# The 32-row tail matmuls of split products on 128 rows, 32 of them with zero weights, in place of 96 rows

## The chip, the cores and the metric

The kernel runs on one core of one Trainium2 chip. The metric is the device time of one execution in microseconds. Before the change it is 1619.23 us, the median of three runs (1618.24 to 1619.66).

## The reference

`x` is 2048 x 576. A layer norm gives `xn`; two branches work on it, and the result is `x + s * silu(b)`.

```python
xn = _layernorm(x, axis=-1)
s = _A_ref(xn, A_wqkv, A_w_phi, A_wo)
g = _silu(_B_ref(xn, B_w_gate, B_w_up, B_w_down))
return x + s * g
```

`_A_ref` is linear attention with 32 heads of 18 columns: `q`, `k` and `v` by one product with `wqkv` (576 x 1728); a feature map for `q` and `k`, which is a small product per head and two softmaxes of it, of both signs; then `phi_q (phi_k^T v)` over a denominator, and a product with `wo` (576 x 576). `_B_ref` is a gated feed-forward part: `(silu(xn @ w_gate) * (xn @ w_up)) @ w_down`, with 4608 hidden columns.

## The kernel before

**Split products.** Each float32 operand is held as a high part, rounded to the type float32r in which TensorE multiplies, and a low part, the rest. A product is then three matmuls: high by high, high by low, low by high. The contraction runs over 576 = 4 x 128 + 64 rows. The kernel cuts it into two blocks `k`, each with two chunks of 128 rows and a tail of 32. A chunk takes three matmuls. A tail takes one: its 32 rows are laid out three times, one copy under the other, with the parts so arranged (the high part in two groups of 32 rows and the low part in the third, on either side in a different group) that one matmul on 96 rows sums the three products. The layout in memory has a fourth copy, in rows 96 to 127, which no matmul reads. So a product of one block is 7 matmuls: six on 128 rows and, as the last, the tail on 96.

**Where tails stand.** Three helpers issue them:
- `xw` (L84 to L95) for the projections to `q`, `k` and part of `v`, and for the early tiles of the feed-forward part (`early_tile`, L121). It goes through both blocks `k`, so one tail is in the middle of an accumulation and one at its end: for each block L87 to L90 list six pairs, L91 the tail, and L94 issues all.
- `v_product` (L412 to L418) for the rest of `v`.
- `product` (L749 to L753) for the gate and up products. `b` is a part of `x` as the moving operand, 512 columns; the weights are the stationary one.

**The feed-forward part** takes most of the time. A unit is one tile of 128 hidden columns for one half of the rows of `x`. Its gate and up products on two blocks of rows are done by a scheme of seven products in place of eight (`gate_up`, L774), each with `product`: `px`, `py` and `pw` (at the start also `pd`) are the PSUM banks they accumulate in. Between products `fill()` (L1087) issues pieces of the down projection, 6 or 12 matmuls of 288 columns each (`three`, L866 to L871), which write `pd`. `gate_up_weights` (L712) brings the weights of a unit: SP loads `ld` (L720), ScalarE and VectorE split it (`split`, L59 to L61), GpSimd forms sums; in the second half of the rows the split weights come back from memory (`w_dram`). The tails of a unit's seven products, already split, come from `t_dram` into the tile `wt`, 96 rows by 7 x 128 (L736). `wt` is taken from the pool `fw` at each unit, from two buffers in turn (L714).

**Order of the work.** The program is written as a whole, and a scheduler places each instruction on its engine's list by its own estimates; `high_priority` and `issue_after` steer it. In the last stretch of the attention part, the projection by `wo` (`project`, L634, matmuls of L650) and the last early tile (L94) share TensorE, and VectorE forms the low parts `ol` that L650 reads (L61). The pool `fw` is opened after this part in the code, and its tiles lie where tiles of the attention part were, so their first writers wait for the last readers of those.

Of the kernel before, what the change touches and what calls it, by code (L numbers as in the profile page):

```python
# [9 lines left out]
F32 = mybir.dt.float32  # L10
F32R = mybir.dt.float32r
# [7 lines left out]
P = 128  # L19
# [29 lines left out]
def gated_hedgehog_kernel(ctx: ExitStack, tc, x, w_qk, w_v, w_phi, wo, w_gu, w_tail, w_down, ident_in, mask_in, out):  # L49
# [5 lines left out]
    nc = tc.nc  # L55
# [3 lines left out]
    def split(hi, lo, src):  # L59
        nc.scalar.copy(hi, src)  # L60
        nc.vector.tensor_sub(lo, src, hi)  # L61
# [15 lines left out]
    t_dram = dram.tile([TAILS, 4, 3, 32, 7, P], F32, name="t_dram")  # L77
# [6 lines left out]
    def xw(ps, i, j, cols, wh, wl, stationary_x):  # L84
        pairs = []
        for k in range(2):
            b = XB[i][2 * j + k]  # L87
            for c in range(2):
                pairs += [(b[:, c, cols], w[:, k, c]) for w in (wh, wl)]
                pairs += [(b[:, 3 + c, cols], wh[:, k, c])]  # L90
            pairs += [(b[0:96, 2, cols], wh[0:96, k, 2])]  # L91
        for n, (a, b) in enumerate(pairs):
            l, r = (a, b) if stationary_x else (b, a)
            last = nc.tensor.matmul(ps, l, r, start=n == 0, stop=n == len(pairs) - 1)  # L94
        return last  # L95
# [8 lines left out]
    def early_weights(f, *behind):  # L104
        parts = []
        for m in (0, 2):
            raw = epool.tile([P, 2, 3, P], F32, name="raw", bufs=2)
            hi = epool.tile([P, 2, 3, P], F32R, name="wh", bufs=3)
            lo = epool.tile([P, 2, 2, P], F32R, name="wl", bufs=3)
            nc.sync.dma_start(raw, w_gu[f, :, m:m + 2])  # L110
            with ExitStack() as order:
                for b in behind:
                    order.enter_context(tc.issue_after(b.ins))
                with tc.high_priority():
                    rests.append(split_rows(hi, lo, raw))
            parts.append((hi, lo))
        return parts
# [19 lines left out]
    with ExitStack() as att:  # L137
# [17 lines left out]
        with ExitStack() as wst:  # L155
# [245 lines left out]
            def xs(k, n):  # L401
                if n < 4:
                    b, cs = XB[k // 4][n], slice(k % 4 * P, (k % 4 + 1) * P)
                    return [b[:, c, cs] for c in range(5)]
                j = n - 4
                h = his[k, j // 2 * 2]
                return [h[:, j % 2, c] for c in range(3)] + [los[k][:, j, c] for c in range(2)]
# [4 lines left out]
            def v_product(ps, x, w, first, last):  # L412
                wh, wl = vws[w]
                mm = [m for c in range(2) for m in ((x[c], wh[:, c]), (x[c], wl[:, c]), (x[3 + c], wh[:, c]))]
                mm += [(x[2][0:96], wh[0:96, 2])]
                for n, (l, r) in enumerate(mm):
                    nc.tensor.matmul(ps[:, 0:HALF], l, r, start=first and n == 0, stop=last and n == len(mm) - 1,
                                     skip_group_check=True)  # L418
# [44 lines left out]
            for p in range(8):  # L463
                k = (p + 4) % 8
# [26 lines left out]
                x = [xs(k, n) for n in range(8)]  # L491
# [186 lines left out]
        for f, halves in [(1, (0,)), (0, (0,))] + [(f, (1, 0)) for f in range(2, EARLY)]:  # L678
            parts = first_weights.pop() if f == 1 else early_weights(
                f, *{0: read[2 * NT + 1:2 * NT + 2], 2: (read[2 * NT + 3], exps[NT + 1])}.get(f, ()))  # L680
# [3 lines left out]
    fw = ctx.enter_context(tc.tile_pool(name="fw", bufs=1))  # L684
    fp = ctx.enter_context(tc.tile_pool(name="fp", bufs=1, reuse_waits="tile"))
    acc = fp.tile([P, 4, HT // 2, HALF], F32, name="acc")

    def operands(i):

        xo = [None] * 7  # L690
        for n in (0, 6, 3, 1, 5, 4, 2):
            if n < 3:
                j = (0, 1, 3)[n]
                if i:
                    t = xpool.tile([P, 5, BT], F32R, name=f"X0{j}")
                    nc.sync.dma_start(t.bitcast(F32), a_dram[n])
                else:
                    t = XB[0][j]
                xo[n] = [t[:, c] for c in range(5)]
                continue  # L700
            j = n - 3
            t = xpool.tile([P, 5, BT], F32R, name=f"X1{j}")
            parts = 1 if i else 4
            rows = t.bitcast(F32).rearrange("p c n -> p (c n)").rearrange("p (a m) -> p a m", a=parts)
            src = sum_dram[i, :, j].rearrange("p s c n -> p (s c n)").rearrange("p (a m) -> p a m", a=parts)
            for a in range(parts):
                nc.sync.dma_start(rows[:, a], src[:, a])
            v = t.rearrange("p c n -> p (c n)").rearrange("p (s c n) -> p s c n", s=4, c=5)
            xo[n] = [v[:, :, c] for c in range(5)]
        return xo  # L710

    def gate_up_weights(i, f):  # L712

        parts, wt = {}, fw.tile([96, 7, P], F32R, name="wt", bufs=2)  # L714
        n, q = divmod(f - EARLY, 4)
        raw = i == 0 or f < FIRST[0]
        if raw:
            ld = fw.tile([P, 2, D], F32, name="ld", bufs=2).rearrange("p a b -> p (a b)")
            ld = ld[:, 0:8 * P].rearrange("p (m c n) -> p m c n", m=4, c=2)
            nc.sync.dma_start(ld, w_gu[f, :, :, 0:2])  # L720
            ts = fw.tile([P, D], F32, name="ts")[:, 0:4 * P].rearrange("p (m c n) -> p m c n", m=2, c=2)

        def ready(m, src):
            k = 1 if m == 6 else 2
            w = fw.tile([P, k, 4, P], F32R, name=f"w{k}", bufs=2 if k == 1 else 4)
            if not raw:
                nc.sync.dma_start(w.bitcast(F32), w_dram[f - EARLY, :, m:m + k])
            else:
                split(w[:, :, 0:2], w[:, :, 2:4], src)
                if i == 0 and f < NF - 1:  # L730
                    nc.sync.dma_start(w_dram[f - EARLY, :, m:m + k], w.bitcast(F32))
            for c in range(k):
                parts[m + c] = w[:, c]

        ready(0, ld[:, 0:2] if raw else None)
        nc.sync.dma_start(wt.bitcast(F32), t_dram[n, q].rearrange("b r m n -> (b r) m n"))  # L736
        if raw:
            nc.gpsimd.tensor_sub(ts[:, 0], ld[:, 2], ld[:, 0])  # L738
            nc.gpsimd.tensor_sub(ts[:, 1], ld[:, 3], ts[:, 0])
            nc.gpsimd.tensor_sub(ld[:, 2], ld[:, 3], ld[:, 2])  # L740
            nc.gpsimd.tensor_sub(ld[:, 1], ld[:, 1], ts[:, 1])  # L741
        ready(4, ts if raw else None)
        ready(2, ld[:, 2:4] if raw else None)
        held = {0: silus[-2:-1], 2: tops[0:1], 3: tops[1:2]}.get(f - FIRST[0]) if i == 0 else None
        with tc.issue_after(held[0].ins) if held else ExitStack():
            ready(6, ld[:, 1:2] if raw else None)
        return parts, wt

    def product(ps, w, m, b, first, last):  # L749
        mm = [(w[0][m][:, i], b[j]) for c in range(2) for i, j in ((c, c), (2 + c, c), (c, 3 + c))]  # L750
        mm += [(w[1][:, m], b[2][0:96])]
        for n, (l, r) in enumerate(mm):
            nc.tensor.matmul(ps, l, r, start=first and n == 0, stop=last and n == len(mm) - 1, skip_group_check=True)  # L753

# [19 lines left out]
    def gate_up(w, xo, fill, opening):  # L774
# [26 lines left out]
        def top(s2):  # L801
            with tc.high_priority():
                anchor.append(nc.vector.tensor_mul(h[0], yp, s2))  # L803

        product(xp, w, 0, A11, True, False)
        with tc.high_priority():
            copies.append(nc.scalar.copy(yp, xp))  # L807
        product(wp, w, 4, S1, True, False)
        if opening < 2:
            product(xp, w, 5, S2, False, False)  # L810
            s2 = snap(xp)
            product(yp, w, 1, A12, False, True)
            silu_y()
            product(xp, w, 2, S3, False, False)
            s3 = snap(xp)
            add(wp, s3)
            add(wp, s2)
            zp = fps.tile([P, 2, 512], F32, name="pd", bufs=2)[:, 0]
            product(zp, w, 3, S4, True, True)
            add(zp, s2)  # L820
            top(s2)
            product(xp, w, 6, A22, False, True)
            silu_x(s3)
            return h
# [274 lines left out]
    parts = early_weights(EARLY)  # L1099
# [11 lines left out]
    for i, n, f in units:  # L1111
# [3 lines left out]
        if f >= FIRST[i]:  # L1115
            w = kept.pop() if i and kept else ready.pop(0)
# [33 lines left out]


def chunks(w):
    tails = [np.broadcast_to(w[512 + 32 * k:544 + 32 * k], (4, 32, w.shape[1])).reshape(P, -1) for k in range(2)]
    return np.stack([np.stack([w[256 * k:256 * k + P], w[256 * k + P:256 * k + 2 * P], tails[k]], 1)
                     for k in range(2)], 1)

# [25 lines left out]
```

## Time and profile before

| what | before |
|---|---|
| median of three runs | 1619.23 us |
| span of the profiled execution, first to last instruction | 1616.8 us |
| time of that execution beside the span | not given by the profile; the median is 2.4 us above the span |
| busy: PE, weight loads, VectorE, ScalarE, GpSimd | 99%, 88%, 72%, 45%, 41% |
| granted TensorE clock, mean | 0.999 |
| DMA, mean | 166 GB/s |

PE stands for matmuls and PEld for the weight loads that overlap them. Records of matmuls overlap each other as well: a matmul's record lasts longer than the time until the next one starts. The span divides roughly into preparation and attention up to 485 us, the first half of the feed-forward part up to some 1040 us, and the second half.

### The profile page before, as it was taken

What the parts mean: (1) busy time and instruction counts of PE and PEld (TensorE: products, weight loads), DVE (VectorE), ACT (ScalarE), POOL (GpSimd) and SP (SyncE); (2) the same over time, 40 slices, a digit from 0 to 9 for tenths busy, and PEclk for the clock granted to TensorE, in tenths of its full rate; (3) what the DMA queues carried; (4) which work ended last, traced back from release to release, by engine and by line L of the source; (5) the groups of instructions that cost most, each with busy time, mean ns of one, the idle gap of its engine ahead of it and who ended that gap; (6) DMA issues with size and microseconds to landing.
All of it is one profiled execution on the core that took longest, in us unless ns stands there. A gap on an engine that the chain in (4) does not pass through costs nothing.

```text
span 1616.8 us, 25312 instructions
## 1 busy us (share of the span) xinstructions
PE 1606.6 (99%) x9415; PEld 1428.7 (88%) x9415; DVE 1171.1 (72%) x1727; ACT 726.1 (45%) x1404; POOL 664.2 (41%) x714
## 2 busy tenths in 40 slices
PE   9999999999999999999999999999999999999998
PEld 6899998999988888888888888888888888888887
DVE  7777769899856778887777778635667656666577
ACT  5633344544435645444444444454343333333334
POOL 3666652334115635644545435223324324133133
PEclk9999999999999999999999999999999999999999
DMA  9522243436447554555555453965545665565445
GB/s 321 183 75 89 98 144 105 119 109 187 128 155 253 175 171 165 178 172 176 176 172 191 167 188 114 335 212 148 152 136 152 191 174 157 169 179 184 142 116 176
DMA packets 123181, 268.29 MB, mean 166 GB/s; under 512 B 12978, under 2 KB 54066, under 8 KB 121778
## 3 DMA queue, kind: packets, MB, share of 16 engines
q1 hardware_dynamic: 107612, 244.73, 46.4%
q0 software_dynamic: 3552, 12.59, 2.7%
q10 hardware_dynamic: 11894, 9.35, 1.8%
q8 instruction: 74, 1.21, 0.3%
q14 instruction: 49, 0.40, 0.1%
HBM read 167.53 MB, written 99.09 MB: 165 GB/s over the span
## 4 chain that ended last, share of the span: by engine, by line
PE 68%; DVE 1%; POOL 1%; DMA 1%; issue 0%; ACT 0%; SPq 0%; DVEq 0%; POOLq 0%
PE px L753 25%; PE pd L870 24%; PE pw L753 12%; PE py L753 6%; POOL acc L900 0%; DMA hb<-h_dram 0%; DVE hh L61 0%; PE pe L94 0%; DMA out<-acc 0%; DVE w L61 0%; POOL ha L1001 0%; PE pd L753 0%; DVE s L787 0%; POOL hb L996 0%; DVE ha L803 0%
## 5 line engine op out<-in xcount | busy, mean ns | idle before, releaser
L870 PEld LDWEIGHTS pd<-dw,hh 128*128 128x128 f32 x3012 | 427.8, 188 | 23.1 <-ACT pd L917 1.5
L870 PE MATMUL pd<-dw,hh 128*128 128x288 f32 x3012 | 443.7, 297 | 1.4 <-ACT pd L917 0.7
L753 PE MATMUL px<-X,w 128*128 128x512 f32 x1512 | 390.4, 393 | 0.0
L753 PEld LDWEIGHTS px<-X,w 128*128 128x128 f32 x1512 | 275.0, 188 | 52.7 <-ACT s L782 2.2
L753 PE MATMUL pw<-X,w 128*128 128x512 f32 x744 | 191.8, 393 | 0.0
L753 PEld LDWEIGHTS pw<-X,w 128*128 128x128 f32 x744 | 139.2, 188 | 31.0
L787 DVE TENSOR_TENSOR s<-pw,s 128x512 f32<-128x512 f32 x126 | 86.5, 688 | 100.4 <-ACT s L782 88.9
L1024 DVE TENSOR_TENSOR acc<-pd,acc 128x576 f32<-128x576 f32 x128 | 96.3, 753 | 84.4 <-PE pd L870 84.3
L782 ACT COPY s<-px 128x512 f32<-128x512 f32 x126 | 73.9, 586 | 160.5 <-PE px L753 160.4
L61 DVE TENSOR_TENSOR hh<-ha,hh 128x512 fp32r<-128x512 f32 x140 | 108.3, 800 | 22.8 <-ACT hh L60 21.3
L60 ACT CAST hh<-ha 128x512 fp32r<-128x512 f32 x140 | 82.7, 619 | 89.2 <-PE pd L870 72.4
L996 POOL TENSOR_TENSOR hb<-hb 128x512 f32<-128x512 f32 x34 | 45.9, 1351 | 164.4 <-DVE hb L799 159.1
L94 PE MATMUL pe<-X,wh 128*128 128x512 f32 (+1 forms) x340 | 108.3, 399 | 0.1
L61 DVE TENSOR_TENSOR w<-ld,w 128x512 fp32r<-128x512 f32 (+1 forms) x96 | 80.8, 844 | 37.2 <-ACT w L60 35.9
L753 PE MATMUL px<-X,wt 96*128 96x512 f32 x252 | 99.5, 395 | 0.0
L753 PE MATMUL py<-X,w 128*128 128x512 f32 x378 | 98.0, 394 | 0.0
L983 POOL TENSOR_TENSOR h<-ha,hb 128x512 f32<-128x512 f32 x34 | 44.7, 1314 | 125.7 <-DVE ha L803 95.5
L1009 POOL TENSOR_TENSOR ha<-ha 128x512 f32<-128x512 f32 x34 | 52.5, 1562 | 98.5 <-DVE hh L61 98.5
L60 ACT CAST w<-ld 128x512 fp32r<-128x512 f32 (+1 forms) x96 | 52.6, 549 | 88.1 <-POOL ld L741 56.0
L807 ACT COPY py<-px 128x512 f32<-128x512 f32 x63 | 36.0, 572 | 106.7 <-PE px L753 86.6
L738 POOL TENSOR_TENSOR ts<-ld 128x256 f32<-128x256 f32 x32 | 27.3, 854 | 130.4 <-issue 68.5
L753 PEld LDWEIGHTS py<-X,w 128*128 128x128 f32 x378 | 67.8, 188 | 11.3
(285 smaller groups left out, 3258.9 us busy)
## 6 DMA issues: line engine op xcount, KB each, us to landing
w_dram<-w SPq DMA_DIRECT2D x90, 512.0 KB
w<-w_dram SPq DMA_DIRECT2D x90, 512.0 KB
wt<-t_dram SPq DMA_DIRECT2D x62, 336.0 KB
ld<-in_B_w_gu SPq DMA_DIRECT2D x32, 512.0 KB
rt<-in_B_w_down SPq DMA_DIRECT2D x33, 288.0 KB
rb<-in_B_w_down SPq DMA_DIRECT2D x33, 288.0 KB
w_dram<-w SPq DMA_DIRECT2D x30, 256.0 KB
w<-w_dram SPq DMA_DIRECT2D x30, 256.0 KB
```

Source lines behind the costliest of these rows:

```text
L60: nc.scalar.copy(hi, src)
L61: nc.vector.tensor_sub(lo, src, hi)
L94: last = nc.tensor.matmul(ps, l, r, start=n == 0, stop=n == len(pairs) - 1)
L753: nc.tensor.matmul(ps, l, r, start=first and n == 0, stop=last and n == len(mm) - 1, skip_group_check=True)
L782: snaps.append(nc.scalar.copy(t, ps))
L787: nc.vector.tensor_add(t, ps, t)
L807: copies.append(nc.scalar.copy(yp, xp))
L870: nc.tensor.matmul(ps, l, r, start=first and n == 0 and m == 0, stop=n == len(hs) - 1 and m == 2, skip_group_check=True)
L983: sub(s, g["h"][0][0], g["h"][0][1])
L996: nc.gpsimd.tensor_add(a21, a21, g["h"][1][1])
L1009: sub(a12, a12, g["h"][0][0])
L1024: nc.vector.tensor_add(a2, pd[:, :, 0:HALF], a2)
```

## The change

All tail matmuls take 128 rows. So that the added 32 rows add nothing, their weights are zero: `chunks`, which lays out the inputs, puts zeros in place of the fourth copy of each weight tail, and `wt` becomes two fixed tiles of 128 rows whose rows 96 to 127 VectorE clears once. `x` keeps its fourth copy. The DMA from `t_dram` still writes 96 rows. The two tiles are used in turn as the two buffers were.

```diff
@@ xw
-            pairs += [(b[0:96, 2, cols], wh[0:96, k, 2])]
+            pairs += [(b[:, 2, cols], wh[:, k, 2])]
@@ v_product
-                mm += [(x[2][0:96], wh[0:96, 2])]
+                mm += [(x[2], wh[:, 2])]
@@ after the pools fw and fp
+    wts = [fw.tile([P, 7, P], F32R, name=f"wt{k}") for k in range(2)]
+    for wt in wts:
+        nc.vector.memset(wt[96:128].bitcast(F32), 0.0)
@@ gate_up_weights
-        parts, wt = {}, fw.tile([96, 7, P], F32R, name="wt", bufs=2)
+        parts, wt = {}, wts[0]
+        wts.reverse()
...
-        nc.sync.dma_start(wt.bitcast(F32), t_dram[n, q].rearrange("b r m n -> (b r) m n"))
+        nc.sync.dma_start(wt[0:96].bitcast(F32), t_dram[n, q].rearrange("b r m n -> (b r) m n"))
@@ product
-        mm += [(w[1][:, m], b[2][0:96])]
+        mm += [(w[1][:, m], b[2])]
@@ chunks
-    tails = [np.broadcast_to(w[512 + 32 * k:544 + 32 * k], (4, 32, w.shape[1])).reshape(P, -1) for k in range(2)]
+    tails = [np.concatenate([w[512 + 32 * k:544 + 32 * k]] * 3 + [np.zeros_like(w[0:32])]) for k in range(2)]
```

In the lists of ScalarE, GpSimd and SP the order of the instructions is as it was. Two lists differ, both near the end of the attention part.

VectorE, before: the last low parts of the attention output, then the split of the first unit's weights (`w` from `ld` and from the sums `ts`).

```order
L132 TENSOR_TENSOR h<-pe,h 128x512
L61 TENSOR_TENSOR ol<-po,oh 126x256
L61 TENSOR_TENSOR ol<-po,oh 72x256
L61 TENSOR_TENSOR w_5326<-ld,w_5326 128x2x256
L61 TENSOR_TENSOR w_5335<-ts,w_5335 128x2x256
```

The same place now:

```order
L132 TENSOR_TENSOR h<-pe,h 128x512
L61 TENSOR_TENSOR ol<-po,oh 126x256
L689 MEMSET wt_5218 32x896
L61 TENSOR_TENSOR ol<-po,oh 72x256
L689 MEMSET wt_5219 32x896
L61 TENSOR_TENSOR w_5329<-ld,w_5329 128x2x256
L61 TENSOR_TENSOR w_5338<-ts,w_5338 128x2x256
```

The two memsets stand on either side of the last `ol`. The first of them holds the wait for PE (the last matmuls that form `po`) which the split of `w` held before, and which SP's first `ld` holds in both.

TensorE, before: the projection's matmuls for the last head group (`ol` and `oh` with 72 rows) and the last early tile (`pe`).

```order
L650 MATMUL p_4547<-WOH,oh 128x288
L650 MATMUL p_4547<-WOL,oh 128x288
L650 MATMUL p<-WOH,oh 128x288
L650 MATMUL p<-WOL,oh 128x288
L650 MATMUL p_4547<-WOH,ol 128x288
L650 MATMUL p<-WOH,ol 128x288
L94 MATMUL pe<-X_60,wh 128x512 x2
```

The same place now:

```order
L650 MATMUL p_4547<-WOH,oh 128x288
L650 MATMUL p_4547<-WOL,oh 128x288
L650 MATMUL p<-WOH,oh 128x288
L650 MATMUL p<-WOL,oh 128x288
L94 MATMUL pe<-X_60,wh 128x512 x2
L94 MATMUL pe<-X_60,wl 128x512
L650 MATMUL p_4547<-WOH,ol 128x288
L650 MATMUL p<-WOH,ol 128x288
L94 MATMUL pe<-X_60,wh 128x512 x2
```

Three matmuls of the early tile now stand ahead of the two that read the last `ol`; they come from the early tile's pieces that stood further down. From the first unit of the feed-forward part on, TensorE's order is the same.

## Prediction

> **What bounds the kernel now.** I read the page's busy shares and its chain of waits first, then the busy time by stage, then single matmuls in order of time.
>
> ```profile
> span 1616.8 us, 25312 instructions
> ...
> PE 1606.6 (99%) x9415; PEld 1428.7 (88%) x9415; DVE 1171.1 (72%) x1727; ACT 726.1 (45%) x1404; POOL 664.2 (41%) x714
> ...
> PE px L753 25%; PE pd L870 24%; PE pw L753 12%; PE py L753 6%; POOL acc L900 0%; DMA hb<-h_dram 0%; DVE hh L61 0%; PE pe L94 0%; DMA out<-acc 0%; DVE w L61 0%; POOL ha L1001 0%; PE pd L753 0%; DVE s L787 0%; POOL hb L996 0%; DVE ha L803 0%
> ```
>
> TensorE is busy 99% of the span, and the chain is almost wholly matmuls: the products of L753 and the down projection of L870. The table by stage shows the same of the two halves of the feed-forward part (columns: stretch, its length, then busy time with instruction counts of PE, PEld, DVE, ACT and POOL, the granted clock, the DMA share, GB/s).
>
> ```profile
> 487.00:1040.00 553.00, 552.29 (x3000) 484.97 (x3000) 429.86 (x607) 273.68 (x541) 274.79 (x261) 1.00 0.54 185
> 1040.00:1595.00 555.00, 555.00 (x3027) 488.17 (x3026) 345.79 (x499) 218.17 (x426) 164.38 (x136) 1.00 0.55 166
> ```
>
> Of 1108 us, PE has no record running in 0.7, and the granted clock is 1.00. So the time is a sum of spacings from one matmul's start to the next one's. No wait can be won here; what counts is by how much a spacing changes where a 96-row tail stands. (Records overlap, so "busy" is no spacing; I take spacings from starts.)
>
> How many tails there are, and what their weight loads take against those of full rows:
>
> ```profile
> L753 PE MATMUL px<-X,wt 96*128 96x512 f32 x252 | 99.5, 395 | 0.0
> L753 PE MATMUL pw<-X,wt 96*128 96x512 f32 x124 | 49.0, 395 | 0.0
> L94 PE MATMUL pe<-X,wh 96*128 96x512 f32 x68 | 26.9, 398 | 0.0
> L753 PE MATMUL py<-X,wt 96*128 96x512 f32 x63 | 24.8, 394 | 0.0
> L94 PE MATMUL p<-QH,X 96*128 96x288 f32 x64 | 19.1, 298 | 0.0
> L94 PE MATMUL p<-KVWH,X 96*128 96x288 f32 x64 | 19.0, 297 | 0.0
> ```
> ```profile
> L753 PEld LDWEIGHTS px<-X,w 128*128 128x128 f32 x1512 | 275.0, 188 | 52.7 <-ACT s L782 2.2
> L753 PEld LDWEIGHTS px<-X,wt 96*128 96x128 f32 x252 | 47.3, 188 | 10.3
> ```
>
> L753 has 252 + 124 + 63 tails, with two more in pd 441. L94 has 68 + 64 + 64 and a few in small groups; with those of L417 I count some 260. A load of 96 rows and one of 128 both take 188 ns.
>
> **The change, part by part.**
>
> *The tails of L753.* Matmuls in order of time, two units of the first half (start, length of the merged rows, then what):
>
> ```profile
> 911.71 0.40 PE L753 MATMUL px<-X,wt 96*128 96x512 f32 x1
> 911.94 1.77 PE L870 MATMUL pd<-dw,hh 128*128 128x288 f32 x12
> 913.54 1.56 PE L753 MATMUL px<-X,w 128*128 128x512 f32 x6
> 914.94 0.39 PE L753 MATMUL px<-X,wt 96*128 96x512 f32 x1
> 915.17 1.78 PE L870 MATMUL pd<-dw,hh 128*128 128x288 f32 x12
> 916.79 1.52 PE L753 MATMUL px<-X,w 128*128 128x512 f32 x6
> 918.15 0.40 PE L753 MATMUL px<-X,wt 96*128 96x512 f32 x1
> 918.38 1.54 PE L753 MATMUL pw<-X,w 128*128 128x512 f32 x6
> 919.77 0.40 PE L753 MATMUL pw<-X,wt 96*128 96x512 f32 x1
> 920.00 1.77 PE L870 MATMUL pd<-dw,hh 128*128 128x288 f32 x12
> 921.60 1.56 PE L753 MATMUL px<-X,w 128*128 128x512 f32 x6
> 923.00 0.39 PE L753 MATMUL px<-X,wt 96*128 96x512 f32 x1
> 923.24 1.53 PE L753 MATMUL pw<-X,w 128*128 128x512 f32 x6
> 924.60 0.40 PE L753 MATMUL pw<-X,wt 96*128 96x512 f32 x1
> 924.83 1.36 PE L870 MATMUL pd<-dw,hh 128*128 128x288 f32 x9
> ```
>
> A tail's own spacing (its start to the next group's): 0.23, 0.23, 0.23, 0.23, 0.24, 0.23, mean 0.232 us. A full matmul's, from the six of a product: 1.40, 1.36, 1.39, 1.40 and 1.36 us for six, so 0.2267 to 0.2333, mean 0.230. The tail costs what its neighbours cost. The step down to 96 rows lies inside those sixes (the sixth full matmul's spacing ends at the tail's start) and shows nothing. The step up could hide in two places. In the tail's own spacing there is at most 0.232 - 0.2267 = 5 ns above the cheapest six. In the product behind it: the two that follow a tail directly (918.38, 923.24) took 1.39 and 1.36 us, the three that follow full-row matmuls of L870 took 1.40, 1.36 and 1.40. A product behind a tail is not the slower one.
>
> *Tails inside an accumulation.* An early tile (L94) has its first tail in the middle of one product, with no change of bank or wait around it:
>
> ```profile
> 40.85 0.63 PE L94 MATMUL pe<-X,wh 128*128 128x512 f32 x2
> 41.32 0.40 PE L94 MATMUL pe<-X,wl 128*128 128x512 f32 x1
> 41.55 0.86 PE L94 MATMUL pe<-X,wh 128*128 128x512 f32 x3
> 42.25 0.40 PE L94 MATMUL pe<-X,wl 128*128 128x512 f32 x1
> 42.49 0.63 PE L94 MATMUL pe<-X,wh 128*128 128x512 f32 x2
> ```
>
> By the order in the code (L87 to L91), each three holds a full matmul, the tail and the next full one; the rows are merged under the first one's shape. The three with both steps takes 42.25 - 41.55 = 0.70 us, 0.233 each; the two and the single without a step take 0.47 and 0.23, 0.233 each. Both steps together cost nothing that 10 ns would show.
>
> So removing the steps is worth between 0 (the L94 rows) and 5 ns (the product ends) for each of 441 tails: 0 to 2.3 us; for the other 260 I allow up to 2 ns, 0.5 us. The L94 rows are nearest, since there only the rows differ, while at a product's end the next load also waits on a semaphore and changes bank. I take 1 ns for 441: -0.5 us. On the other side, a 128-row tail that costs more than a 96-row one is bounded by the largest spacing among full-row matmuls, 0.2333 against 0.232: +0.6 us.
>
> Here a rule of the Trainium skill can be weighed, after the rows: they show a step of rows at 0.23 us, which is the ordinary spacing. "TensorEngine Tiling (Array Packing)", section Tiling Modes, Key Properties, says that a change of tiling mode (not of the tile alone) drains TensorE. If 96 rows counted as another mode, the sum would hold two drains for each tail; by these rows it holds none.
>
> *The two memsets on VectorE.* They clear rows 96 to 127 of both wt tiles, 896 elements each, once. The order puts the first ahead of the last `ol` subtraction of the attention part, with the wait for PE that SP's first `ld` has too, and the second behind that subtraction.
>
> ```profile
> 466.49 0.40 PE L630 MATMUL po<-pl,KVH 72*72 72x256 f32 x2
> 467.98 0.42 PE L650 MATMUL p<-WOH,ol 72*128 72x288 f32 x2
> 468.24 0.63 PE L94 MATMUL pe<-X,wh 128*128 128x512 f32 x2
> ```
> ```profile
> 467.33 0.42 DVE L61 TENSOR_TENSOR ol<-po,oh 72x256 fp32r<-72x256 f32 x1 [1.53 <-ACT oh L60]
> 473.27 0.78 DVE L61 TENSOR_TENSOR w<-ld,w 128x512 fp32r<-128x512 f32 x1 [5.53 <-ACT w L60]
> ```
> ```profile
> 466.92 0.58 SPq L720 DMA_DIRECT2D ld<-in_B_w_gu  x1
> ```
> ```profile
> L304 DVE MEMSET v<- 128x4 f32 x2 | 0.1, 62 | 0.0
> ```
>
> No memset of this size is in the trace. From below: 62 ns for 4 elements. From above: 0.42 us for the 256 elements of `ol`, which also reads two operands, so 896 / 256 x 0.42 = 1.5 us. I take 1.3, near the upper end, because the size is nearer to that row. Released at about 466.9, it ends near 468.2; `ol` then runs to 468.6 in place of 467.75, 0.9 us late. The matmuls that read it (467.98) stand behind three early-tile matmuls that the new order has put ahead of them: 3 x 0.233 = 0.70 us, so PE has work to 468.68. Cost: 0 to 0.1 us; without that cover 0.9. The second memset falls into the 5.5 us in which VectorE waits ahead of 473.27. SP's list is the same but for names, and the DMA into wt still writes 96 rows. The three matmuls are moved, not added.
>
> *The rest* (the zero rows in the weights' layout, 128 rows in L94 and L417) alters no size of a DMA, copy or subtraction: the tail chunk already had 128 rows.
>
> Sum: -0.5 + 0.1 = -0.4 us on the span of 1616.8. The profile gives no time beside the span; the median, 1619.23, stands 2.4 us above it, and I leave that as it is. 1619.2 - 0.4 = 1618.8.
>
> **The rivals.**
>
> *Steps cost more than I read (faster).* Suppose each step up disturbs its neighbours as well: own spacing 5 ns for some 700 tails, 3.5 us, and the product directly behind a tail, where there are about 200 (most tails are followed by L870), at 1.39 in place of 1.36 us: up to 6.0 us. With half of the second, 6.5 us: 1612.7; with a quarter of it, 5 us: 1614.2. For it: the tails are never the cheapest spacing. Against: 923.24 directly behind a tail is as cheap as any, and 913.54 and 921.60 are dear without one.
>
> *Each step drains the array (much faster).* A matmul's record lasts 0.40 us and the next starts after 0.23. If the array emptied at each step, 0.17 us would be lost twice for each tail: 441 x 0.33 = 146 us, and the time would be 1473. Against it speaks every tail above. (This is what the skill's page would give if 96 rows were a mode of its own.)
>
> *The 128-row tail is dearer (slower).* Its load takes 32 more partitions' data, and the first load behind a product's end must wait for it. If the tail's spacing rose from 0.232 to 0.240, the largest single reading (923.00 to 923.24), 441 x 0.008 = 3.5 us: 1622.7. It decides from 7.3 ns a tail (3.2 / 441). Against: full rows load in the same 188 ns and stand at 0.230 on average.
>
> **How the numbers follow.** A measurement here can tell about 0.2%, 3.2 us, from no change. My forecast, spacings as they are, gets 0.72; its own range is 1619.2 - 2.3 - 0.5 = 1616.4 to 1619.2 + 0.6 + 0.9 = 1620.7, all inside 0.2%. Dearer steps get 0.20, the drain 0.01, the dearer tail 0.07. So faster 0.21, same 0.72, slower 0.07. The range runs from 1613.5, in the midst of the first rival, to 1620.7: it leaves out the slower case, the drain and the larger part of what the first rival could give at most.
>
> **What would show it.** The tail rows must read 128*128 and 188 ns. Right: in the same stretch, tails at 0.23 us to the next group and sixes between 1.36 and 1.40; span within 3 us. The first rival is right if the groups behind tails fall to 1.36 throughout; the slower one if tails stand at 0.24. The memset is mis-sized if PE shows idle time ahead of the `ol` matmuls near 468 us. I am wrong as a whole if the spacings stay and the span still moves by over 3 us: then something outside the tails has changed.

## The result, and the profile after

The changed kernel takes 1604.64 us, the median of four runs (1604.21 to 1605.32); the kernel before 1619.45 us (the three executions given above and one more). The ratio is 0.991, with a 95% interval of 0.9898 to 0.9922. It is faster by some 14.8 us, outside the range that was given. One execution of all those below, of the second experiment's kernel, was slow (2232.53 us at a granted clock of 0.654); its ratio leaves that one out, and its median without it is 1617.95 us.

Of the page of the changed kernel: the span, TensorE's share, and the two costliest groups of matmuls (busy time is the time covered by a group's records). L757 and L874 are the lines L753 and L870 of before.

```profile
span 1602.3 us, 25315 instructions
...
PE 1590.9 (99%) x9414; PEld 1421.0 (89%) x9415; DVE 1170.6 (73%) x1729; ACT 725.1 (45%) x1404; POOL 665.8 (42%) x714
...
L874 PE MATMUL pd<-dw,hh 128*128 128x288 f32 x3012 | 438.3, 295 | 1.2 <-ACT pd L921 0.7
L757 PE MATMUL px<-X,w 128*128 128x512 f32 x1512 | 386.3, 390 | 0.0
```

TensorE is as full as before, in a span that is 14.5 us shorter, with as many matmuls (9414 records against 9415). So the matmuls follow each other faster, and not the tails alone. The two groups of the kernel before:

```profile
L870 PE MATMUL pd<-dw,hh 128*128 128x288 f32 x3012 | 443.7, 297 | 1.4 <-ACT pd L917 0.7 <-DVE X L1024 0.4 <-DVE hh L61 0.3
L753 PE MATMUL px<-X,w 128*128 128x512 f32 x1512 | 390.4, 393 | 0.0
```

The down projection, in which the change touches nothing, covers 5.4 us less. By stage, the whole gain lies behind 487 us: in the same two windows TensorE now starts 97 more matmuls (3045 + 3079 against 3000 + 3027), at the same granted clock.

```profile
487.00:1040.00 553.00, 552.50 (x3045) 488.47 (x3044) 430.71 (x610) 276.47 (x547) 276.14 (x262) 1.00 0.54 189
1040.00:1595.00 555.00, 554.33 (x3079) 491.32 (x3079) 353.40 (x513) 225.13 (x442) 171.13 (x143) 1.00 0.55 167
```

The weight loads of the tails in `px`: 128 rows, and 188 ns as before.

```profile
L757 PEld LDWEIGHTS px<-X,wt 128*128 128x128 f32 x252 | 47.3, 188 | 9.9
```

The stretch that answers to the one of before, matmuls in order of time:

```profile
907.36 1.53 PE L757 MATMUL px<-X,w 128*128 128x512 f32 x6
908.73 0.39 PE L757 MATMUL px<-X,wt 128*128 128x512 f32 x1
908.95 1.75 PE L874 MATMUL pd<-dw,hh 128*128 128x288 f32 x12
910.53 1.53 PE L757 MATMUL px<-X,w 128*128 128x512 f32 x6
911.90 0.39 PE L757 MATMUL px<-X,wt 128*128 128x512 f32 x1
912.12 1.52 PE L757 MATMUL pw<-X,w 128*128 128x512 f32 x6
913.49 0.39 PE L757 MATMUL pw<-X,wt 128*128 128x512 f32 x1
913.71 1.75 PE L874 MATMUL pd<-dw,hh 128*128 128x288 f32 x12
```

In these rows six full matmuls take 1.37 us wherever they stand; before it was 1.36 to 1.40. A tail stands 0.22 us ahead of the next group, before 0.23 or 0.24. Twelve of the down projection take 1.58 us (908.95 to 910.53), before 1.60 to 1.62.

The rows have a grain of 10 ns. From the starts of all matmuls in the trace I worked out the median spacing by place, in ns; "t" marks the tail, and a run is two products followed by twelve matmuls of the down projection. The rows below "after" are kernels of the experiments.

```
                 product behind L870/L874      product behind a product      the twelve
before           238 233 235 225 231 235 t233  232 227 227 227 227 227 t233  134 133 138 135 133 133 134 128 132 130 139 134
after            231 227 227 227 227 227 t227  227 227 227 227 227 227 t227  128 133 132 136 136 131 131 132 129 131 131 132
tail as fourth   231 227 227 t233 237 233 231  227 227 227 t233 237 233 231  128 133 133 136 136 131 131 132 129 131 131 132
all on 96 rows   234 232 231 227 227 227 t227  227 227 227 227 227 227 t227  133 131 132 133 132 132 136 136 131 131 133 129
tail on 112      238 233 235 225 231 235 t233  232 227 227 227 227 227 t232  134 133 138 135 133 133 134 128 132 130 139 134
two steps        238 233 235 233 232 231 t232  238 232 234 233 232 231 t232  134 133 138 135 133 134 134 127 132 130 139 134
tail on 64       232 231 227 227 227 318 t428  333 227 227 227 227 318 t428  234 133 128 132 131 132 133 133 132 136 136 131
32 bytes on      230 235 231 235 232 235 t232  234 232 235 232 235 232 t235  131 131 131 133 132 132 134 135 131 132 133 130
```

A median hides that the spacings of before come in two patterns. They part when the tails are sorted by what stands ahead of them: regular, where the last two full matmuls ahead of the tail have 229 ns or less, or upset.

```
before, tail and then a product:         tail, then the six full matmuls (median ns)
  ahead regular (80 tails)               t232  238 232 231 227 227 227
  ahead upset (127 tails)                t233  232 227 227 227 227 227
before, tail, twelve and then a product: the twelve, then the six full matmuls (us)
  ahead regular (127 tails)              1.60  1.40   (in 124 and 122 of them)
  ahead upset (43 tails)                 1.62  1.36   (in 42 and 42 of them)
```

Behind a regular product the tail and the next three matmuls have 25 or 26 ns over 227, in all 80 cases. Behind an upset one it is 10 or 11 ns in 81 of 127 cases, and 25 or 26 in 18.

Summed over the span, the spacings of the 2646 full matmuls of the products fall from 611.5 to 605.0 us, those of the 441 tails from 102.9 to 100.1, those of the down projection from 410.6 to 405.2: together 14.6 us (the unrounded sums), which is the gain. L94 has 260.7 before and 260.8 after: nothing.

### The profile page after: what moved, and what is told of

It is laid out like the page before. It is cut to its first block, busy times and chain, and to the rows that moved or that the text cites. A ratio compares the mean times of both kernels' runs of the same rounds, so it can differ in the third digit from the quotient of the medians.

```text
span 1602.3 us, 25315 instructions
## 1 busy us (share of the span) xinstructions
PE 1590.9 (99%) x9414; PEld 1421.0 (89%) x9415; DVE 1170.6 (73%) x1729; ACT 725.1 (45%) x1404; POOL 665.8 (42%) x714
## 4 chain that ended last, share of the span: by engine, by line
PE 93%; DMA 2%; POOL 2%; DVE 1%; ACT 1%; issue 1%; SPq 0%; DVEq 0%; POOLq 0%; ACTq 0%
PE px L757 25%; PE pd L874 24%; PE pw L757 12%; PE p L94 6%; PE py L757 6%; PE pe L94 5%; PE p L650 4%; PE kvp L329 2%; PE po L630 2%; PE vx L417 1%; PE pt L624 1%; POOL slo L362 1%; DMA h_dram<-h 1%; PE tp L248 1%; PE vy L94 1%
## 5 line engine op out<-in xcount | busy, mean ns | idle before, releaser
L874 PEld LDWEIGHTS pd<-dw,hh 128*128 128x128 f32 x3012 | 423.8, 188 | 22.1 <-ACT pd L921 1.5
L874 PE MATMUL pd<-dw,hh 128*128 128x288 f32 x3012 | 438.3, 295 | 1.2 <-ACT pd L921 0.7
L757 PE MATMUL px<-X,w 128*128 128x512 f32 x1512 | 386.3, 390 | 0.0
L757 PEld LDWEIGHTS px<-X,w 128*128 128x128 f32 x1512 | 274.5, 188 | 48.9 <-ACT s L786 2.3
L757 PE MATMUL pw<-X,w 128*128 128x512 f32 x744 | 190.4, 391 | 0.0
L757 PEld LDWEIGHTS pw<-X,w 128*128 128x128 f32 x744 | 138.6, 188 | 29.1
L94 PE MATMUL pe<-X,wh 128*128 128x512 f32 x340 | 108.4, 400 | 0.5 <-ACT wh L64 0.5
L757 PE MATMUL px<-X,wt 128*128 128x512 f32 x252 | 98.0, 389 | 0.0
L757 PE MATMUL py<-X,w 128*128 128x512 f32 x378 | 97.0, 391 | 0.0
L757 PEld LDWEIGHTS py<-X,w 128*128 128x128 f32 x378 | 67.8, 188 | 10.6
```

Of the source, the lines that this page charges most:

```text
L874: nc.tensor.matmul(ps, l, r, start=first and n == 0 and m == 0, stop=n == len(hs) - 1 and m == 2, skip_group_check=True)
```

## The experiments

Where no ratio is given, the time is that of one execution. Thirteen executions of the kernel before, in one round, lie between 1617.44 and 1620.74 us, so in those cases the spacings say more than a microsecond of time does.

The theory after the result (S): a change in the number of rows between matmuls upsets the beat of what follows for several matmuls, and this aftermath is the loss. Rivals: the two fixed `wt` tiles and other waits bring the gain (T); the tails of L94 and L417 have a part in it (A); a 96-row matmul is dear by itself (R); the step costs only at a product's end (B).

**The products' tails alone on 128 rows.** L94 and L417 go back to 96.

```diff
-            pairs += [(b[:, 2, cols], wh[:, k, 2])]
+            pairs += [(b[0:96, 2, cols], wh[0:96, k, 2])]
...
-                mm += [(x[2], wh[:, 2])]
+                mm += [(x[2][0:96], wh[0:96, 2])]
```

> The changed kernel with the tails of L94 and L417 back on 96 rows; those of the gate and up products stay on 128. Theory S (each step from 96 to 128 rows upsets the spacing of what follows, in the feed-forward part alone): the whole gain stays, 1604 to 1606 us. Theory A (the tails of L94 and L417 bring part of it): 1607 to 1612. Theory T (the two fixed wt tiles and the new waits bring the gain, not the rows): 1604 to 1606 here too, told apart by the second kernel.

Measured: 1605.5 us, ratio to before 0.9915 (0.9899 to 0.9932). The gain stays.

**The other tails alone on 128 rows**, with fixed tiles and memsets kept.

```diff
-        mm += [(w[1][:, m], b[2])]
+        mm += [(w[1][0:96, m], b[2][0:96])]
```

> The changed kernel with the gate and up products' tails reading rows 0 to 95 of the fixed wt tiles; L94 and L417 on 128 rows, the memsets kept. Theory S: the gain is gone, 1618 to 1620 us, full matmuls of the products at 231 ns on average again. Theory A: 1612 to 1616. Theory T: the gain stays, 1604 to 1606.

Measured: 1618.24 us (median of all ten), ratio 0.9997 (0.9987 to 1.0006). The gain is gone. Both kernels have the same order of instructions as the changed one on every engine. T and A fall: it is the rows of the products' tails.

**The tail as the fourth matmul of a product** (on the kernel before).

```diff
-        mm += [(w[1][:, m], b[2][0:96])]
+        mm.insert(3, (w[1][:, m], b[2][0:96]))
```

> The kernel before, with the 96-row tail as the fourth matmul of a gate or up product in place of the last. Theory S: a step inside an accumulation upsets what follows as one at its end does, 1616 to 1622 us. Theory B (it is the step together with the end of a product: new bank, new wait): the loss shrinks, 1604 to 1611.

Measured: 1617.2 us. B falls. Matmuls in order of time:

```profile
903.54 0.85 PE L753 MATMUL px<-X,w 128*128 128x512 f32 x3
904.22 0.40 PE L753 MATMUL px<-X,wt 96*128 96x512 f32 x1
904.45 0.86 PE L753 MATMUL px<-X,w 128*128 128x512 f32 x3
905.15 0.84 PE L753 MATMUL pw<-X,w 128*128 128x512 f32 x3
```

The three full matmuls ahead of the tail take 0.68 us, the three behind it 0.70. In the table the aftermath stands by itself: the tail and the next three have 233, 237, 233 and 231, then 227 again. That is 6 + 10 + 6 + 4 = 26 ns for each tail, 11.5 us for 441. In this kernel the aftermath is over before the down projection starts, and the twelve have the same spacings as in the changed kernel.

**All seven matmuls of a product on 96 rows.**

```diff
         mm += [(w[1][:, m], b[2][0:96])]
+        mm = [(l[0:96], r[0:96]) for l, r in mm]
```

> The kernel before, with all seven matmuls of a gate or up product on 96 rows (it leaves out rows 96 to 127 of the full chunks). Theory S: steps are left only where a product is followed by matmuls of the down projection, about 240 of 441; the time falls to 1606 to 1614 us, and a product that follows a product runs at 227 ns throughout. Theory R (a 96-row matmul is dear by itself, some 6 ns and what it does to the next): seven times as many of them, slower than before by 15 us or more.

Measured: 1607.8 us. R falls: seven times as many matmuls on 96 rows, and faster than before by some 11 us.

```profile
903.47 1.54 PE L754 MATMUL py<-X,w 96*128 96x512 f32 x6
904.85 0.39 PE L754 MATMUL py<-X,wt 96*128 96x512 f32 x1
905.08 1.52 PE L754 MATMUL px<-X,w 96*128 96x512 f32 x6
906.44 0.39 PE L754 MATMUL px<-X,wt 96*128 96x512 f32 x1
```

Here `py` follows the down projection, with a step of rows, and takes 1.38 us for six; `px` follows `py` without one and takes 1.36. So a step down upsets the beat too: 234, 232, 231 against 231, 227, 227. The step up, into the down projection, shows as well: its twelve take 1.589 us (median) against 1.583 in the changed kernel.

**A second step in each product** (on the kernel before).

```diff
         mm += [(w[1][:, m], b[2][0:96])]
+        mm[2] = tuple(t[0:96] for t in mm[2])
```

> The kernel before, with the third matmul of each gate or up product on 96 rows as well as the tail (it leaves out rows 96 to 127 of that chunk). The run with the tail as fourth shows 26 ns for a step inside a product (6, 10, 6 and 4 ns over 227 in the tail's and the next three spacings). Theory S: a second step adds some 441 x 26 ns = 11 us to before, 1626 to 1632 us. Theory U (once upset, the spacing is not upset further): 1617 to 1621.

Measured: 1627.24 us, 8.6 us over before (1618.67 beside it), or 19 ns for each added step there and back. U falls for the kernel as a whole. But the steps do not simply add up: behind a product the six matmuls ahead of the tail go from a median of 1381 to 1401 ns, behind the down projection, where the beat was upset already, only from 1398 to 1403.

**The tail on 64 rows.**

```diff
-        mm += [(w[1][:, m], b[2])]
+        mm += [(w[1][0:64, m], b[2][0:64])]
```

> The changed kernel with the product tails on 64 rows (it leaves out the third group of 32 rows of each tail). If it is the fact of a step that costs: as before, 1616 to 1620 us. If the cost grows with the rows that are switched: 1622 to 1635.

Measured: 1775.42 us. Neither number was near.

```profile
900.19 1.53 PE L757 MATMUL px<-X,w 128*128 128x512 f32 x6
901.65 0.50 PE L757 MATMUL px<-X,wt 64*128 64x512 f32 x1
902.08 1.63 PE L757 MATMUL pw<-X,w 128*128 128x512 f32 x6
903.63 0.50 PE L757 MATMUL pw<-X,wt 64*128 64x512 f32 x1
904.06 1.85 PE L874 MATMUL pd<-dw,hh 128*128 128x288 f32 x12
```
```profile
901.65 0.18 PEld L757 LDWEIGHTS px<-X,wt 64*128 64x128 f32 x1 [0.35 <-issue]
902.08 1.21 PEld L757 LDWEIGHTS pw<-X,w 128*128 128x128 f32 x6 [0.24 <-issue]
```

The spacings around such a tail are 318, 428 and 333 ns in place of 227: 398 ns, or 176 us for 441; the time rose by 170.8 us over the changed kernel. The built program gives a 64-row matmul another tile size than a 128-row one, and 96 and 112 rows the same as 128. The weight loads stop for 0.35 us ahead of the tail's load, which starts only with the tail's own row (901.65), and for 0.24 us behind it; in the kernel before a 96-row tail's load (914.71) starts 0.23 us ahead of its matmul (914.94). This is a loss of another kind, and it fits the prediction's rival of a drained array. The Trainium skill's page "TensorEngine Tiling (Array Packing)", Tiling Modes, Key Properties, says that a change of mode drains TensorE, and the trace agrees for 64 rows, as far as a stop of loads and matmuls can show a drain. For 96 rows, which are no mode of the page, the runs show 26 ns and no such stop.

**The tail on 112 rows**, 16 of them with zero weights.

```diff
-        mm += [(w[1][:, m], b[2])]
+        mm += [(w[1][0:112, m], b[2][0:112])]
```

> The changed kernel with the product tails on 112 rows, 16 of them with zero weights. Theory G (what costs is that a group of 32 rows falls idle and comes back): as the changed kernel, 1604 to 1606 us, tails at 227 ns. Theory N (any step in the count of rows costs): 1616 to 1620, tails at 233.

Measured: 1618.16 us (before beside it 1618.23).

```profile
899.84 1.54 PE L757 MATMUL pw<-X,w 128*128 128x512 f32 x6
901.22 0.40 PE L757 MATMUL pw<-X,wt 112*128 112x512 f32 x1
901.45 1.77 PE L874 MATMUL pd<-dw,hh 128*128 128x288 f32 x12
```

All of the loss is back, with the spacings of before at nearly every place. G falls: a step of 16 rows costs what one of 32 does.

**The added rows without zeros.**

```diff
-        nc.vector.memset(wt[96:128].bitcast(F32), 0.0)
+        nc.vector.memset(wt[96:128].bitcast(F32), 0.01)
```

> The changed kernel with rows 96 to 127 of the wt tiles set to 0.01 in place of 0 (the sum then holds a term that does not belong to it). If the row count brings the gain: 1604 to 1606 us. If the zeros do (less switching in the array): 1610 or more.

Measured: 1604.27 us, with the spacings of the changed kernel. The zeros bring nothing; the count does.

**Why L94 gained nothing.** In the changed kernel the matmuls of L94 with 512 columns have no step left and still stand at 231 to 238 ns, never at 227 for long. In the built program the weights of the early tiles start 32 bytes off a multiple of 64; those of the products start at multiples of 64. A pad moves the former:

```diff
+    epool.tile([P, 24], F32, name="pad", bufs=1)
     est.close()
...
-        idle = const.tile([P, BT], BF16, name="idle")
+        idle = const.tile([P, 448], BF16, name="idle")
...
-                nc.tensor.matmul(unused, idle[:, 0:P], idle, start=True, stop=True)
+                nc.tensor.matmul(unused[:, 0:448], idle[:, 0:P], idle, start=True, stop=True)
```

> The changed kernel with a pad of 96 bytes in the pool of the early tiles, so that their weights (and the parts of the sums that L417 reads) start at multiples of 64 bytes; the idle matmuls at the start are cut from 512 to 448 columns to make room. Theory P: matmuls of L94 with 512 columns go from 234 to 227 ns, 504 of them, 3 to 4 us faster than the changed kernel, 1600 to 1602. If the place does not matter: 1604 to 1606, L94 at 234.

Measured: 1604.41 us, ratio to before 0.9911 (0.9894 to 0.9927): the same as the changed kernel, where 1600 to 1602 was expected. The spacing did change. First the changed kernel, then this one (a group of three is again a full matmul, the tail and the next full one):

```profile
479.47 0.64 PE L94 MATMUL pe<-X,wh 128*128 128x512 f32 x2
479.94 0.39 PE L94 MATMUL pe<-X,wl 128*128 128x512 f32 x1
480.18 0.86 PE L94 MATMUL pe<-X,wh 128*128 128x512 f32 x3
480.88 0.39 PE L94 MATMUL pe<-X,wl 128*128 128x512 f32 x1
```
```profile
479.33 0.62 PE L94 MATMUL pe<-X,wh 128*128 128x512 f32 x2
479.78 0.39 PE L94 MATMUL pe<-X,wl 128*128 128x512 f32 x1
480.01 0.84 PE L94 MATMUL pe<-X,wh 128*128 128x512 f32 x3
480.69 0.39 PE L94 MATMUL pe<-X,wl 128*128 128x512 f32 x1
```

Two take 0.45 us in place of 0.47, three 0.68 in place of 0.70; the median goes from 234 to 228. Of what these matmuls read, only the weights have moved, by 96 bytes. Why the time did not follow is not shown. One candidate stands at the start: the idle matmuls are shorter, the granted clock from 11 to 16 us is 0.66 (1.00 in the changed kernel), and the first transposes are late. The row of the first full block, in this kernel:

```profile
11.31 4.37 PE L215 MATMUL tp<-ident,xn 128*128 128x128 f32 x22 [0.20 <-POOL xn L206]
```

In the changed kernel these 22 take 2.92 us. But the order of some instructions near the start has changed too, and this profile is of the slowest of four executions (1606.05 us, the others 1603.82 to 1604.62).

**The steps put back into the aligned early tiles.**

```diff
-            pairs += [(b[:, 2, cols], wh[:, k, 2])]
+            pairs += [(b[0:96, 2, cols], wh[0:96, k, 2])]
```

> The kernel with aligned early tiles, with the tails of L94 back on 96 rows. Theory P (steps cost nothing in L94 before because its spacing was upset by the weights' place already): with that cleared, each tail shows again, about 26 ns: matmuls of L94 with 512 columns go from a median of 227 or 228 to one of 230 or more, with the 233, 237, 232, 231 after each tail that the gate and up products showed. Otherwise they stay at 227.

Measured: median spacing in L94 233 in place of 228 (1605.14 us, one run).

```profile
479.96 0.62 PE L94 MATMUL pe<-X,wh 128*128 128x512 f32 x2
480.42 0.39 PE L94 MATMUL pe<-X,wl 128*128 128x512 f32 x1
480.64 0.86 PE L94 MATMUL pe<-X,wh 128*128 128x512 f32 x3
481.34 0.40 PE L94 MATMUL pe<-X,wl 128*128 128x512 f32 x1
```

The three with the tail in it takes 0.70 us again, the two without stays near 0.45 (0.46). By the starts, the tail and next three have 233, 237, 233 and 231, the very numbers of the products. P holds: L94 hid its steps, because its beat was upset anyway.

**The products' weights moved off.** The reverse of that:

```diff
+    fw.tile([P, 8], F32, name="pad", bufs=1)
     wts = [fw.tile([P, 7, P], F32R, name=f"wt{k}") for k in range(2)]
```

> The changed kernel with a pad of 32 bytes ahead of the wt tiles, so that all tiles of the feed-forward pools lie 32 bytes further on (their addresses were multiples of 64 bytes). Theory P (the early tiles stand at 234 ns with and without steps because their weights lie 32 bytes off a multiple of 64): full matmuls of the products go from 227 to 234 ns, 3087 of them, 1624 to 1630 us with what the down projection adds. If the place does not matter: 1604 to 1606.

Measured: 1621.1 us, 16.5 us over the changed kernel, on 128 rows throughout; less than was expected.

```profile
903.98 1.55 PE L758 MATMUL px<-X,w 128*128 128x512 f32 x6
905.37 0.40 PE L758 MATMUL px<-X,wt 128*128 128x512 f32 x1
905.61 1.56 PE L758 MATMUL pw<-X,w 128*128 128x512 f32 x6
907.01 0.40 PE L758 MATMUL pw<-X,wt 128*128 128x512 f32 x1
```

Six take 1.39 and 1.40 us. The down projection, whose operands moved too, has 133.3 ns on average against 133.0: it does not mind.

**Aligned early tiles and a longer start**, the version that this points to.

```diff
-                keep_clock(31)
+                keep_clock(36)
...
-                    keep_clock(6)
+                    keep_clock(7)
```

> The kernel with aligned early tiles, with 36 and 7 idle matmuls of 448 columns at the start in place of 31 and 6. In the run without this the first transposes ran at the low clock (22 of them in 4.37 us against 2.92) and the start was some 1.5 us late. If that ate the gain of the aligned early tiles: 1601 to 1603 us, faster than the changed kernel by 1.5 to 3 us. If the matmuls of the early tiles were not on the path: 1604 to 1605.

Measured: 1603.58 us (1602.7 to 1604.37), ratio to before 0.9907 (0.989 to 0.9923). The time lies between the two forecasts. The 22 transposes take 2.91 us again, and the spacings of L94 with 512 columns sum to 120.8 us against 122.7; other kernels whose early tiles are those of the changed one have 121.4 to 122.6, and the aligned one without the longer start 122.0. So what the aligned weights are worth there is at most some 2 us and not cleanly sized. The median is 1.1 us under the changed kernel's, but the intervals overlap and the profiled span is 0.3 us longer: whether it is faster, and whether the start ate the gain before, is not settled.

## Why the prediction was wrong, point by point

- *What bounds the kernel* was right: a sum of spacings, no wait, and the gain is in spacings alone.
- The step that failed is "The tail costs what its neighbours cost". It was true of the rows and no measure of the tail: the neighbours carried its aftermath. The term that it gave the sum, 1 ns for each of 441 tails or 0.5 us, measures 14.6 us by the spacings, 33 ns for each. The mean of 0.230 us that served as the ordinary spacing was itself 3 ns too high, and the sixes of 1.39 and 1.40 were no scatter, but the tail's work. The cheapest six, 1.36, was the floor, and 2646 full matmuls could fall to it.
- "A product behind a tail is not the slower one" compared products directly behind a tail with products behind the down projection, and took the latter as undisturbed. But the down projection itself stands behind a tail. Single spacings in the prediction's own rows show what mixed the readings. The six from 918.38 have 238, 232, 231 and then 227, the whole aftermath of a tail, since the product ahead (916.79) ran regular; the six from 923.24 are spared (231, then 227), since the product ahead (921.60: 238, 234, 235, 225, 230, 236) was upset already. And 916.79 is cheap where the twelve ahead of it took 1.62 us in place of 1.60. These are the two patterns sorted out under the table, and the prediction's five sixes held some of each.
- "Both steps together cost nothing that 10 ns would show" in L94 was right as a reading. It failed as a control: L94 was upset for another reason, and with that removed the steps show there with the same 26 ns. It was called the nearest row because only the rows differ in it; that an undisturbed L94 might stand below 233 was not considered.
- The first rival named the mechanism, and both of its terms were about right in size: 3.5 us for the tails' own spacing (2.7 measured, all at L753), and up to 6.0 us for products directly behind a tail, of which it took a quarter to a half (3.0 measured, over 207 products). It left out what the tail does to the down projection (5.4 us) and to the products behind that (3.7 us over 224). Its sign came: behind tails the sixes now stand at 1.36 to 1.37 us.
- The drain was rightly refused for 96 rows; with 64 rows a loss of its kind comes, 398 ns where the price worked out from overlapping records was 0.33 us.
- The dearer tail is refuted: 227 ns on 128 rows.
- The memsets were sized at 1.3 us and take 0.81; their cover was read rightly. VectorE, then TensorE, in the changed kernel:

```profile
467.59 0.81 DVE L689 MEMSET wt<- 32x896 f32 x1 [1.34 <-PE po L630]
468.43 0.42 DVE L61 TENSOR_TENSOR ol<-po,oh 72x256 fp32r<-72x256 f32 x1
```
```profile
468.44 0.63 PE L94 MATMUL pe<-X,wh 128*128 128x512 f32 x2
468.90 0.39 PE L94 MATMUL pe<-X,wl 128*128 128x512 f32 x1
469.14 0.43 PE L650 MATMUL p<-WOH,ol 72*128 72x288 f32 x2
```

The last `ol` ends at 468.85, and the three moved matmuls keep TensorE going to 469.14. It was released later than was read, at 467.59 and not 466.9.

What stays open is why a step upsets the beat, why it does so for just the next three matmuls where the beat is regular and for longer behind it in the down projection, and why an upset beat hides part of a step. No run separates the step down from the step up at a tail; the kernel with all seven on 96 rows does so only at the borders with the down projection, where both show.

## What to carry to other kernels

Where TensorE is full and matmuls of 512 columns follow each other, give all of them the same number of rows, the full 128, with zero or otherwise harmless weights in the added ones, and let the weights start at multiples of 64 bytes (only starts at 0 and 32 bytes past one were tried; what that is worth in time showed in the products, 16.5 us in one execution, and not clearly in the early tiles). To price such a thing, don't hold the suspect against its neighbours: look for the smallest spacing that occurs in the trace for that shape, ask what every larger one has in common, and count the whole stream down to it. A stretch in which the suspect shows no cost is a control only if that stretch runs at the floor.

## What the runs showed of the hardware that was not expected

- One tail with another count of rows than its neighbours, 96 or 112 against 128, costs 26 ns in a regular stream of 512-column matmuls (6, 10, 6, 4), and mostly 10 or 11 in a stream that is upset already, though its weight load takes the same 188 ns and no gap shows in the records. The Trainium skill, "TensorE: Matmul & The Clock Gate", LDWEIGHTS (loading the stationary operand), says that the count of rows does not matter for a load; the trace agrees for the load's length, and the spacing differs all the same.
- Weights that start 32 bytes off a multiple of 64 put a 512-column matmul at some 234 ns in place of 227, in two different parts of the kernel. Matmuls of 288 columns showed no such thing.
- A 64-row matmul between 128-row ones, built with a tile of 64 rows, costs 398 ns, and the weight loads stop on both sides of it.
- Seven 96-row matmuls in a row run at the same 227 ns as 128-row ones.
